# Query and key features stored feature first and head second, with one norm product for queries and one for keys per block

## The chip, the cores and the metric

The kernel runs on one core of one Trainium2 chip. A core has TensorE (PE in the profile, with its weight loads as PEld), VectorE (DVE), ScalarE (ACT), GpSimd (POOL) and SyncE (SP), which issues most DMAs. The metric is the device time of one execution in microseconds (us); the time of a kernel is the median of its runs.

## The reference

Two layers with the same weights act on 2048 tokens of 448 features: attention of 16 heads of 28 features, then a gated unit of 1792 features, each behind a layer norm without parameters and each added to its input.

```python
B, S, D, H, F = 1, 2048, 448, 16, 1792
def _A_ref(x, wqkv, wo):
    Dh = D // H                                           # 28
    qkv = (x @ wqkv).reshape(B, S, 3, H, Dh).transpose(2, 0, 3, 1, 4)
    q, k, v = qkv[0], qkv[1], qkv[2]
    scores = jnp.einsum("bhqd,bhkd->bhqk", q, k) * (Dh ** -0.5)
    o = jnp.einsum("bhqk,bhkd->bhqd", _softmax(scores), v)
    return o.transpose(0, 2, 1, 3).reshape(B, S, D) @ wo
def _B_ref(x, w_gate, w_up, w_down):
    return (_sigmoid(x @ w_gate) * (x @ w_up)) @ w_down
for layer in range(2):
    x = x + _A_ref(_layernorm(x), wqkv, wo)
    x = x + _B_ref(_layernorm(x), w_gate, w_up, w_down)
```

The columns of `wqkv` are ordered query, key, value; within each the head comes first and the feature within the head second. All inputs are float32.

## The kernel before

**Stages.** Each layer has a projection (`project`), the attention of 16 heads, the output projection and the gated unit. The change lies in the projection, and in the reads and writes that connect it to the weights before it and the heads behind it.

**Order of work.** Nothing plans the order at run time. Each engine executes its instructions in the order in which the program issues them, and waits on semaphores for its operands, so a waiting instruction holds all that stand behind it on its engine. The author interleaves work by hand: lists of small functions (`fill`, `along`, `along_values`) say what is issued between one tile and the next.

**Precision.** Activations and weights are kept as pairs of f16, a high part and the rest. A product of float32 quality is made of three f16 products: high by high, high by low, low by high.

**The projection's queries and keys.** The tokens come in 4 blocks of 512 (`W`). In a block, `qk` makes the 896 query and key features in 7 tiles of 128 features: tiles 0 to 2 hold queries, tile 3 holds the last 64 query features and the first 64 key features, tiles 4 to 6 hold keys. For each tile, `by_features` (L564) issues eleven matmuls of 512 columns into one of four PSUM banks. Then ScalarE writes the high part (L756), VectorE the low part (L757), both into `qkhl`; ScalarE squares the high part into `sq`, in bf16 (L759); VectorE takes the maximum of the left and right half of the 512 tokens (L761), which leaves 256 columns; and SyncE stores `qkhl` to `qk_scr` in DRAM (L764).

**The norms.** The softmax uses a bound from the largest norms of queries and keys. The squares of the 28 features of a head are summed by a product with a table of zeros and ones, `ind`. With the head first, every tile has features of other heads, so each tile has its own columns of the table: four products gather the query norms in one bank (L735) and four the key norms in another (L738), tile 3 going into both. The products stand in a queue `late`. From the fourth tile on, the oldest is issued behind the current tile's matmuls:

```python
if len(late) == 3:
    late.popleft()()
```

so those of tile 2 stand behind tile 5. The rest are issued by `finish` (`fin()`), in blocks 0 and 1 behind a value product, in block 2 between the first tiles of block 3, in block 3 behind the first value product that follows it. `finish` also reduces the two banks to `peaks` on VectorE. `tables` builds `ind` on GpSimd.

**The value products** (L589 to L591) follow the tiles of blocks 0 and 1; those of blocks 2 and 3 follow block 3's tiles. Beside all of it the norms of later blocks are computed on VectorE (`norm`, `squares`, `scale` at L320), their rows are transposed through DRAM and loaded back (`gather`), and split into parts (`ready`: the high part at L218 on ScalarE, the low one at L219 on VectorE). Block 1 of layer 0 is transposed on TensorE instead (L508, `turn`), behind VectorE's scaling at L320.

**The weights.** In layer 0 the weights come as float32 and are split on the chip: `high_cols` scales and rounds columns on ScalarE (L231), `low_cols` makes the rest on VectorE (L234). A power of two for the scale comes from a sum of squares (`measure`, `size`, with `powers` at L246 and L248). The first query columns are split before the first tile, the others between the first tiles of block 0 (`tile0`, `tile1`, `tile2`). The parts are written to DRAM (`keep`) and read back for layer 1 (`load`), so layer 1 splits nothing.

**The heads.** `HeadOperands.load` (L681 to L689) reads a head's 28 features from `qk_scr`, both parts of queries and keys, in several transfers on SyncE's queue. The scores are products of these rows (L1207).

Of the kernel before, what the change touches and what calls it, by code (L numbers as in the profile page):

```python
# [118 lines left out]
def interleaved_layers(ctx: ExitStack, tc: tile.TileContext, x_in, wqkv, wo, w_gate, w_up,  # L119
# [39 lines left out]
    ind_f = qrt.get("ind_f", [P, 8, H])  # L159
# [27 lines left out]
    def tables():  # L187


        nc.gpsimd.memset(ind_f, 1.0)  # L190
        for j in range(2):
            v = ind_f[:, 4 * j:4 * j + 4, :]
            off = -64 * j
            nc.gpsimd.affine_select(out=v, in_=v, compare_op=ALU.is_ge, fill=0.0, base=off,
                                    pattern=[[P, 4], [-DH, H]], channel_multiplier=1)
            nc.gpsimd.affine_select(out=v, in_=v, compare_op=ALU.is_ge, fill=0.0,
                                    base=DH - 1 - off, pattern=[[-P, 4], [DH, H]],
                                    channel_multiplier=-1)
        nc.gpsimd.memset(ind[:, 8:, :], 0.0)
        nc.gpsimd.tensor_copy(ind[:, 0:8, :], ind_f)  # L200
        qrt.put(ind_f)
# [24 lines left out]
    def scaled_high(hi, raw, m, engine=None):  # L226
        by = up[:, m:m + 1]
        if engine is nc.vector:
            nc.vector.tensor_scalar(hi, raw, by, None, op0=ALU.mult)
        else:  # L230
            nc.scalar.activation(hi, raw, AF.Copy, scale=by)  # L231
# [368 lines left out]
    class WeightsQKV:  # L600
# [37 lines left out]
            nc.tensor.matmul(pb[:, 0:1], ones, sums[:, j:j + 1], start=True, stop=True)  # L638
            powers(j, 1, pb[:, 0:1])

        def high_cols(self, j, c0, c1, kts=slice(0, 4)):
            c = slice(j * D + c0, j * D + c1)
            scaled_high(self.qk[0][:, kts, c], self.raw[j][:, kts, c0:c1], j)

        def low_cols(self, j, c0, c1):
            c = slice(j * D + c0, j * D + c1)
            scaled_low(self.qk[1][:, :, c], self.qk[0][:, :, c], self.raw[j][:, :, c0:c1], j)

        def split_v(self):
            for kts in (slice(0, 2), slice(2, 4)):  # L650
# [13 lines left out]
            nc.sync.dma_start(self.v, v_parts)  # L664


    qk_scr = dpool.tile([2 * D, 2, S], F16, name="qk_scr")
    g_scr = dpool.tile([H, 2, S], F16, name="g_scr")

    class HeadOperands:  # L670
# [8 lines left out]
        def load(self):  # L679
            h, q, k = self.h, self.q, self.k  # L680
            nc.sync.dma_start(k[RQ:RG, :], unit_scr)  # L681
            qs = qk_scr[h * DH:(h + 1) * DH]
            ks = qk_scr[D + h * DH:D + (h + 1) * DH]
            both = "d c n -> (d c) n"
            nc.sync.dma_start(q[0:2 * DH, :], qs.rearrange(both))
            nc.sync.dma_start(k[0:2 * DH, :], ks.rearrange(both))
            nc.sync.dma_start(q[2 * DH:RQ, :], qs.rearrange(both))
            nc.sync.dma_start(k[2 * DH:RQ:2, :], ks[:, 1, :])
            nc.sync.dma_start(k[2 * DH + 1:RQ:2, :], ks[:, 0, :])  # L689

        def load_guard(self):
            nc.sync.dma_start(self.q[RQ:RG, :], g_scr[self.h])
# [19 lines left out]
    def project(layer, wq, begun):  # L712
# [12 lines left out]
        def qk(b, blk, fill, before):  # L725
            pn = [bank(4 + 2 * (b % 2), "qnorm"), bank(5 + 2 * (b % 2), "knorm")]
            late = deque()

            def rows_of_heads(i):

                return ind[:, i:i + P // H, :].rearrange("p a h -> p (a h)")

            def norm_products(i, sq):
                if i <= 3:
                    nc.tensor.matmul(pn[0][:, 0:W // 2], rows_of_heads(i), sq[:, 0:W // 2],  # L735
                                     start=(i == 0), stop=(i == 3))
                if i >= 3:
                    nc.tensor.matmul(pn[1][:, 0:W // 2], rows_of_heads(1 + i), sq[:, 0:W // 2],  # L738
                                     start=(i == 3), stop=(i == 6))
                qrt.put(sq)  # L740

            for i in range(7):
                pm = bank(evac[0] % 4, "qkp")
                evac[0] += 1
                c = slice(i * P, (i + 1) * P)
                by_features(pm, blk, lambda kt: wq.qk[0][:, kt, c],
                            lambda kt: wq.qk[1][:, kt, c], i if layer == 0 and b == 0 else None)
                if layer == 0 and b == 0:
                    along[i]()
                if before and i in (1, 2):  # L750
                    before(i == 2)
# [4 lines left out]
                nc.scalar.activation(hl[:, 0, :], pm, AF.Copy, scale=PS)  # L756
                nc.vector.scalar_tensor_tensor(hl[:, 1, :], pm, PS, hl[:, 0, :], op0=ALU.mult,  # L757
                                               op1=ALU.subtract)
                nc.scalar.activation(sq, hl[:, 0, :], AF.Square)  # L759

                nc.vector.tensor_tensor(sq[:, 0:W // 2], sq[:, 0:W // 2], sq[:, W // 2:W],  # L761
                                        op=ALU.max)
                n = slice(b * W, (b + 1) * W)
                nc.sync.dma_start(qk_scr[c, :, n], hl)  # L764
                qrt.put(hl)
                late.append(lambda i=i, sq=sq: norm_products(i, sq))
                if i < len(fill) and fill[i]:
                    fill[i]()

            def finish(whole=True):  # L770

                while len(late) > (0 if whole else 1):
                    late.popleft()()
                for i in range(2 if whole else 0):
                    nc.vector.tensor_reduce(peaks[:, i, b:b + 1], pn[i][0:H, 0:W // 2], axis=AX.X,
                                            op=ALU.max)
            return finish
# [19 lines left out]
                blk.drop()  # L797

        def tile0():
            wq.low_cols(0, P, D)  # L800
            wq.measure(1)
            ones_of_values()

        def tile1():
            wq.size(1)
            wq.high_cols(1, 0, 64)
            wq.low_cols(1, 0, 64)

        def tile2():
            wq.high_cols(1, 64, D)  # L810
            wq.low_cols(1, 64, D)

        def nothing():
            pass
# [1039 lines left out]
    wq.sum_first(2)  # L1854
    tables()
    keep_busy(3)
    wq.high_cols(0, 0, P, slice(0, 1))
    wq.high_cols(0, 0, P, slice(1, 4))
    first.turned_high([3])
    wq.high_cols(0, P, D)  # L1860
    first.turned_low([1])
    wq.low_cols(0, 0, P)
    first.turned_low([2, 3])
    big.put(first.xn)
    qrt.put(still)
# [40 lines left out]
```

## Time and profile before

| | |
|---|---|
| median of 3 runs | 1894.67 us (1894.47 to 1895.89) |
| profiled execution, its span | 1893.0 us; the page gives it by its span alone |
| TensorE, matmuls | 1886.5 us busy |
| TensorE, weight loads | 1323.1 us |
| VectorE | 1430.7 us |
| ScalarE | 1382.7 us |
| GpSimd | 231.5 us |

The profile is one execution, recorded by the hardware profiler. The page gives busy times by engine and by group of instructions; a group's row has the line, the engine, the operation, output and inputs with their shapes, the count, then busy time, mean duration in ns, and the idle time of the engine just before with what ended it. The rows of the timeline begin with the start in us from the start of the span and a duration; `x3` at the end says that three neighbouring instructions were merged into one row, and a bracket says how long the engine had waited, and for which instruction. Matmuls overlap, so a matmul's duration is longer than the step to the next one.

### The profile page before, as it was taken

Reading aid. Unit: us, or ns where it says so; the run is one execution under the profiler, and the core shown is the slowest. Engines: PE = TensorE matmul, PEld = TensorE weight load, DVE = VectorE, ACT = ScalarE, POOL = GpSimd, SP = SyncE. Lnnn points to the kernel's source line nnn. Section 1 sums busy time; section 2 is a strip of 40 time slices with the busy share of each in tenths; the row PEclk is TensorE's granted clock in tenths of the full one; section 3 lists DMA queues with packets and bytes.
Section 4 is the critical chain, followed back from the end, with each engine's and each line's share of the span. In section 5 each row is a group of like instructions: output and inputs, shape, how many; then the busy total and the mean of one; then the engine's idle time right before and its main releaser. Section 6 shows DMA issues by size and latency. Waiting matters only on the chain. (4 is left out here: it accounts for less than half of the span.)

```text
span 1893.0 us, 56282 instructions
## 1 busy us (share of the span) xinstructions
PE 1886.5 (100%) x24254; PEld 1323.1 (70%) x24254; DVE 1430.7 (76%) x2835; ACT 1382.7 (73%) x1772; POOL 231.5 (12%) x453
## 2 busy tenths in 40 slices
PE   9999999999999999999999999999999999999999
PEld 4455555555556799999954556667666567999998
DVE  7758989898976688787564487787778676887664
ACT  5569999999993566555345799999999745565541
POOL 3023112222101111111100000000000020121110
PEclk9999999999999999999999999999999999999999
DMA  7676454334323566646734322122120245666553
GB/s 247 194 212 166 132 137 128 107 119 129 103 88 121 192 205 235 231 181 238 251 96 134 90 52 47 32 52 52 31 48 24 67 160 174 218 251 223 208 208 142
DMA packets 110882, 270.86 MB, mean 143 GB/s; under 512 B 13214, under 2 KB 67838, under 8 KB 110496
## 3 DMA queue, kind: packets, MB, share of 16 engines
q0 software_dynamic: 31776, 158.51, 23.4%
q1 hardware_dynamic: 78288, 108.20, 20.3%
q8 instruction: 192, 3.15, 0.7%
q10 hardware_dynamic: 560, 0.46, 0.1%
q14 instruction: 66, 0.54, 0.1%
HBM read 207.88 MB, written 50.85 MB: 137 GB/s over the span
## 5 line engine op out<-in xcount | busy, mean ns | idle before, releaser
L1222 ACT ACTIVATE prob_s<-sc 128x1536 f32<-128x1536 f32 (+1 forms) x657 | 887.9, 1487 | 6.6 <-PE sc L1207 5.9
L1258 PE MATMUL acc<-prob_s,val_s 128*32 128x256 f32 (+3 forms) x7700 | 569.9, 383 | 0.0
L1207 PE MATMUL sc<-qp_s 114*32 114x512 f16 x7868 | 553.2, 379 | 0.0
L579 PEld LDWEIGHTS <-gu_s 128*128 128x128 f16 x4368 | 426.9, 98 | 46.8 <-issue 0.4
L1207 PEld LDWEIGHTS <-qp_s 114*32 114x32 f16 x8192 | 272.7, 95 | 203.4 <-issue 88.3
L1258 PEld LDWEIGHTS acc<-prob_s,val_s 128*32 128x32 f32 x7700 | 272.3, 110 | 142.9 <-issue 13.6
L579 PE MATMUL chain<-xwide_s,gu_s 128*128 128x256 f16 x2016 | 247.5, 273 | 0.0
L1552 PE MATMUL dnp<-dn_s,hparts_s 128*128 128x224 f16 x2016 | 225.2, 259 | 0.0
L1552 PEld LDWEIGHTS <-hparts_s 128*128 128x128 f16 x2016 | 194.0, 98 | 4.4
L1238 DVE SCALAR_TENSOR_TENSOR power_q<-power_q,expo_q 128x512 f32<-128x512 f32 x243 | 168.2, 692 | 8.3
L1625 ACT COPY one_q<-chain 128x256 f32<-128x256 f32 x224 | 82.4, 371 | 121.4 <-PE chain L579 120.8
L1641 DVE TENSOR_TENSOR one_q<-side,one_q 128x512 f32<-128x512 f32 x112 | 72.2, 686 | 101.8 <-PE side L579 101.5
L579 PE MATMUL side<-xshort_s,gu_s 128*128 128x256 f16 x1120 | 140.5, 273 | 0.0
L564 PE MATMUL qkp<-xhl_s,wqk_s 128*128 128x512 f16 x616 | 138.1, 379 | 0.7 <-ACT wqk_s L231 0.2
L564 PEld LDWEIGHTS <-wqk_s 128*128 128x128 f16 x616 | 60.1, 98 | 69.8 <-ACT wqk_s L231 1.1
L1437 POOL DMA_DIRECT2D gu_s<-gu_parts x104 | 56.0, 538 | 430.5 <-PE side L579 424.5
L1287 DVE STREAM_TRANSPOSE oturned_q<-acc 128x512 f32<-128x512 f32 x32 | 22.9, 716 | 97.1 <-PE acc L1258 96.9
L1258 PE MATMUL acc<-power_q,val_s 128*32 128x256 f32 (+3 forms) x300 | 94.2, 396 | 0.0
L579 PE MATMUL side<-xwide_s,gu_s 128*128 128x256 f16 x672 | 91.6, 273 | 0.0
L1505 ACT CAST hparts_s<-hsums_q 128x256 f16<-128x256 f32 (+1 forms) x136 | 65.0, 494 | 30.2 <-DVE hsums_q L1517 20.2
L756 ACT ACTIVATE qkhl_q<-qkp 128x512 f16<-128x512 f32 x56 | 33.2, 593 | 71.9 <-PE qkp L564 68.3
L1652 ACT ACTIVATE one_q<-one_q 128x512 f32<-128x512 f32 x56 | 35.2, 629 | 64.3 <-DVE one_q L1641 64.3
(218 smaller groups left out, 2318.0 us busy)
## 6 DMA issues: line engine op xcount, KB each, us to landing
gu_s<-gu_parts POOLq DMA_DIRECT2D x104, 800.0 KB, 6.0
dn_s<-dn_parts POOLq DMA_DIRECT2D x42, 784.0 KB, 7.8
qp_s<-qk_scr SPq DMA_DIRECT2D x96, 224.0 KB
qk_scr<-qkhl_q SPq DMA_DIRECT2D x56, 256.0 KB
gu_parts<-pack_s POOLq DMA_DIRECT2D x14, 800.0 KB, 3.8
xt_scr<-xs_s SPq DMA_DIRECT2D x48, 224.0 KB
xraw_s<-xt_scr SPq DMA_DIRECT2D x12, 768.0 KB
qp_s<-qk_scr SPq DMA_DIRECT2D x64, 112.0 KB
```

The source lines that it names most:

```text
L564: nc.tensor.matmul(pm, w, x, start=(i == 0), stop=(i == len(terms) - 1))
L579: nc.tensor.matmul(pm, a, x, start=(first and i == 0), stop=(i == len(terms) - 1), skip_group_check=True)
L1207: nc.tensor.matmul(ps[32 * j:32 * j + 32, :], hd.k[:, keys], hd.q[:, qb * W:(qb + 1) * W], start=True, stop=True, tile_position=(0, 32 * j))
L1222: nc.scalar.activation(prob[:, 0:n, :], ps[:, 0:n, :], AF.Exp, scale=exp_scale)
L1238: nc.vector.scalar_tensor_tensor(p, p, c[k], y, op0=ALU.add, op1=ALU.mult)
L1258: nc.tensor.matmul(acc[qb * VC:(qb + 1) * VC, s], v[:, kc % TB, h, :], probs[c * NB + qb][:, s], start=(kc == 0 and a == 0), stop=(kc == N ...
L1437: queue.dma_start(self.gu[-1][m], gu_parts[p, m])
L1505: nc.scalar.copy(to[:, :, 0], a)
L1552: nc.tensor.matmul(pm, a[:, x, t], w[:, p, y], start=(begin and n == 0 and (j == 0 or alone)), stop=(n == 2), skip_group_check=True)
L1625: nc.scalar.copy(to, pm)
L1641: nc.vector.tensor_tensor(one[m], side[m], one[m], op=ALU.add)
L1652: nc.scalar.activation(out, v, AF.Sigmoid, scale=gate_scale)
```

## The change

Query and key features are stored with the feature first and the head second: row `d * 16 + h` instead of `h * 28 + d`. Every tile of 128 features then holds 8 features of all 16 heads, row r belonging to head r mod 16 in every tile, so the squares of several tiles can be added row by row before one product with one table.

- `ind` is one 128x128 table with the sums of heads in its first 16 columns; VectorE makes them from the identity matrix in one reduction (`sums_of_heads`) and GpSimd clears the rest.
- `squares_of` replaces `norm_products`. VectorE adds the squares of tiles 1, 2 and the query half of tile 3 to tile 0's, those of tiles 5 and 6 and the key half of tile 3 to tile 4's, over all 512 tokens; it takes the maximum of the two halves once for queries (tile 3) and once for keys (tile 6). One product for each follows. The query product is issued behind tile 5, the key product by `finish`.
- The weights of layer 0 are split with the same instructions, but read with a step of 28 words, and written in the new order; the low part is cut in four instructions, one for each 128 rows of weights. The first pieces are 8 features of 16 heads where 128 columns were.
- `qk_scr` is stored by query or key, part, row and token; tile 3 goes in two stores. A head's rows are 16 rows apart.

```diff
-    ind = cpool.tile([P, 7 + P // H, H], BF16, name="ind")
+    ind = cpool.tile([P, P], BF16, name="ind")
...
+    def sums_of_heads():
+        with nc.allow_low_precision(reason="zeros and a one"):
+            nc.vector.tensor_reduce(ind[:, 0:H], ident.rearrange("p (a h) -> p h a", h=H),
+                                    axis=AX.X, op=ALU.add)
...
-        def high_cols(self, j, c0, c1, kts=slice(0, 4)):
-            c = slice(j * D + c0, j * D + c1)
-            scaled_high(self.qk[0][:, kts, c], self.raw[j][:, kts, c0:c1], j)
-
-        def low_cols(self, j, c0, c1):
-            c = slice(j * D + c0, j * D + c1)
-            scaled_low(self.qk[1][:, :, c], self.qk[0][:, :, c], self.raw[j][:, :, c0:c1], j)
+        def columns(self, j, d0, d1, kts=slice(0, 4)):
+            c = j * D + (0 if j == 0 else -24 * H if d0 == 24 else 64)
+            c = slice(c + H * d0, c + H * d1)
+            hi, lo = [t[:, kts, c].rearrange("p k (d h) -> p k d h", h=H) for t in self.qk]
+            raw = self.raw[j][:, kts].rearrange("p k (h d) -> p k d h", h=H)[:, :, d0:d1]
+            return hi, lo, raw
+
+        def high_cols(self, j, d0, d1, kts=slice(0, 4)):
+            hi, lo, raw = self.columns(j, d0, d1, kts)
+            scaled_high(hi, raw, j)
+
+        def low_cols(self, j, d0, d1):
+            hi, lo, raw = self.columns(j, d0, d1)
+            for kt in range(4):
+                scaled_low(lo[:, kt], hi[:, kt], raw[:, kt], j)
...
-    qk_scr = dpool.tile([2 * D, 2, S], F16, name="qk_scr")
+    qk_scr = dpool.tile([2, 2, D, S], F16, name="qk_scr")
...
+            qs, ks = [rows[:, h] for rows in qk_scr.rearrange("w c (d h) n -> w (c d) h n", h=H)]
+            nc.sync.dma_start(q[0:2 * DH, :], qs)
...
-            def norm_products(i, sq):
-                if i <= 3:
-                    nc.tensor.matmul(pn[0][:, 0:W // 2], rows_of_heads(i), sq[:, 0:W // 2],
-                                     start=(i == 0), stop=(i == 3))
-                if i >= 3:
-                    nc.tensor.matmul(pn[1][:, 0:W // 2], rows_of_heads(1 + i), sq[:, 0:W // 2],
-                                     start=(i == 3), stop=(i == 6))
+            def norm_product(z, sq):
+                nc.tensor.matmul(pn[z][:, 0:W // 2], ind, sq[:, 0:W // 2], start=True, stop=True)
                 qrt.put(sq)
 
+            def squares_of(i, sq):
+                if i in (0, 4):
+                    sums["k" if i else "q"] = sq
+                    if i:
+                        both = sums.pop("both")
+                        nc.vector.tensor_tensor(sq[64:P], sq[64:P], both[64:P], op=ALU.add)
+                        qrt.put(both)
+                    return
+                z = 0 if i <= 3 else 1
+                to = sums["qk"[z]]
+                r = slice(0, 64 if i == 3 else P)
+                nc.vector.tensor_tensor(to[r], to[r], sq[r], op=ALU.add)
+                if i == 3:
+                    sums["both"] = sq
+                else:
+                    qrt.put(sq)
+                if i in (3, 6):
+                    nc.vector.tensor_tensor(to[:, 0:W // 2], to[:, 0:W // 2], to[:, W // 2:W],
+                                            op=ALU.max)
+                    late.append(lambda: norm_product(z, to))
...
-                if len(late) == 3:
+                if late and i in (2, 5):
                     late.popleft()()
...
-                nc.vector.tensor_tensor(sq[:, 0:W // 2], sq[:, 0:W // 2], sq[:, W // 2:W],
-                                        op=ALU.max)
+                squares_of(i, sq)
...
-                while len(late) > (0 if whole else 1):
+                while whole and late:
                     late.popleft()()
```

More of the change, by code (lines that the diff above doesn't have):

```diff
@@ L187, in tables @@
     def tables():
[L190 to L201, printed above, removed]
+        nc.gpsimd.memset(ind[:, H:], 0.0)
         units = big.get("units", [2, S], F16)
@@ L799, in tile0 @@
         def tile0():
-            wq.low_cols(0, P, D)
+            wq.low_cols(0, 8, DH)
+            sums_of_heads()
             wq.measure(1)
@@ L805, in tile1 @@
             wq.size(1)
[L806 to L807 removed]
+            wq.high_cols(1, 24, DH)
+            wq.low_cols(1, 24, DH)
         def tile2():
[L810 to L811 removed]
+            wq.high_cols(1, 0, 24)
+            wq.low_cols(1, 0, 24)
         def nothing():
```

32 lines of the change are left out of this document (15 added, 17 removed).

## The prediction

> **What bounds the kernel now.** I read the page first, then the matmul rows of the projection stage in order of time, then VectorE's rows of the same stretches, to see how far VectorE runs behind TensorE.
>
> ```profile
> span 1893.0 us, 56282 instructions
> PE 1886.5 (100%) x24254; PEld 1323.1 (70%) x24254; DVE 1430.7 (76%) x2835; ACT 1382.7 (73%) x1772; POOL 231.5 (12%) x453
> L735 PE MATMUL qnorm<-sq_q,ind 128*128 128x256 bf16 x32 | 8.7, 272 | 0.0
> L738 PE MATMUL knorm<-sq_q,ind 128*128 128x256 bf16 x32 | 6.4, 273 | 0.0
> ```
>
> TensorE is busy for all but 6.5 us of the span, so work taken off it shortens the kernel, and every wait put into its queue lengthens it. The page gives the profiled execution by its span, 1893.0 us; the median of the runs is 1.7 us above that. I work out a difference on the trace and add it to the median, 1894.67. About 0.2% (3.8 us) is what a measurement can tell from no change.
>
> There are 64 norm products, 8 for each of 4 blocks in 2 layers. What one costs is its step, not its duration, since matmuls overlap:
>
> ```profile
> 100.20 0.27 PE L735 MATMUL qnorm<-sq_q,ind 128*128 128x256 bf16 x1
> 102.68 0.27 PE L735 MATMUL qnorm<-sq_q,ind 128*128 128x256 bf16 x1
> 102.79 0.27 PE L738 MATMUL knorm<-sq_q,ind 128*128 128x256 bf16 x1
> 104.98 0.49 PE L738 MATMUL knorm<-sq_q,ind 128*128 128x256 bf16 x3
> ```
>
> From 102.68 to 102.79 is 0.11 us. The first row is the q product that follows feature tile 5 of block 3 in layer 0; the last holds the three k products that wait until the first value product is done.
>
> **Products.** 64 become 16: 48 x 0.109 = 5.2 us of TensorE, 2.6 in each layer. That is all that the change can give. What remains moves: the q product still stands behind tile 5, but now needs the sum over tiles 0 to 3, where the product there needed tile 2's squares. It is queued ahead of tile 6's eleven matmuls and all that follow.
>
> **VectorE's sums.** Seven maxima of 128x256 go; six adds of 128x512 (two of them on 64 partitions, which takes as long) and two maxima come in each block.
>
> ```profile
> 101.19 0.68 DVE L757 SCALAR_TENSOR_TENSOR qkhl_q<-qkp,qkhl_q 128x512 f16<-128x512 f32 x1
> 101.79 0.28 DVE L761 TENSOR_TENSOR sq_q<-sq_q 128x256 bf16<-128x256 bf16 x1
> 101.99 0.68 DVE L757 SCALAR_TENSOR_TENSOR qkhl_q<-qkp,qkhl_q 128x512 f16<-128x512 f32 x1
> L1516 DVE TENSOR_TENSOR hsums_q<-two_q,one_q 128x256 f32<-128x256 f32 x48 | 20.4, 425 | 1.6
> L761 DVE TENSOR_TENSOR sq_q<-sq_q 128x256 bf16<-128x256 bf16 x56 | 15.9, 284 | 0.0
> ```
>
> Back to back, an eviction holds the engine 0.60 us and a maximum 0.20. In bf16 256 columns last 284 ns, in f32 425, so bf16 goes at two elements a cycle, and a 512-column bf16 add should last 0.42 and hold the engine 0.33; with a maximum that depends on it behind, 0.45. So tile 0 gives VectorE 0.20 back, tiles 1, 2, 4 and 5 cost 0.13 each, tiles 3 and 6 cost 0.45: 1.2 us a block. The sum for q is ready 0.60 + 0.45 + 0.33 = 1.38 us after tile 3's eviction begins.
>
> **Where that meets TensorE.** VectorE's evictions of tile 3 in blocks 1 and 2 of layer 0 and block 1 of layer 1, and the q products behind tile 5:
>
> ```profile
> 58.02 0.65 DVE L757 SCALAR_TENSOR_TENSOR qkhl_q<-qkp,qkhl_q 128x512 f16<-128x512 f32 x1
> 83.47 0.69 DVE L757 SCALAR_TENSOR_TENSOR qkhl_q<-qkp,qkhl_q 128x512 f16<-128x512 f32 x1
> 992.03 0.69 DVE L757 SCALAR_TENSOR_TENSOR qkhl_q<-qkp,qkhl_q 128x512 f16<-128x512 f32 x1
> 56.89 0.27 PE L735 MATMUL qnorm<-sq_q,ind 128*128 128x256 bf16 x1
> 82.71 0.27 PE L735 MATMUL qnorm<-sq_q,ind 128*128 128x256 bf16 x1
> 993.80 0.27 PE L735 MATMUL qnorm<-sq_q,ind 128*128 128x256 bf16 x1
> 32.87 0.94 DVE L320 TENSOR_SCALAR xn_s<-x,mv,rs 128x448 f32<-128x448 f32 x2
> 33.48 1.66 PE L508 MATMUL turn<-ident,xn_s 128*128 128x128 f32 x8
> 37.07 1.04 PE L508 MATMUL turn<-ident,xn_s 128*128 128x128 f32 x8
> 64.31 0.68 DVE L757 SCALAR_TENSOR_TENSOR qkhl_q<-qkp,qkhl_q 128x512 f16<-128x512 f32 x1
> 79.85 1.29 DVE L219 TENSOR_TENSOR xhl_s<-xraw_s,xhl_s 128x512 f16<-128x512 f32 x2 [5.07 <-ACT xhl_s L218]
> ```
>
> In layer 0 VectorE carries the next blocks' norms between the evictions and runs late: at 56.89 TensorE stands behind tile 5 while tile 3's eviction only begins at 58.02. I follow the delay (after less before), the weights' reads being no dearer:
>
> - Block 0. The transposes (33.48, 1.66 us where the next take 1.04) wait for VectorE's scaling at 32.87. The sums of tiles 2, 3 and 5 lie in front of it, 0.13 + 0.45 + 0.13, with 0.04 of splitting (tile 4's hides in a wait for ScalarE): TensorE is 0.75 late there, and its four saved products are lost in the wait. Three k products become one: +0.53 at block 1.
> - Block 1. VectorE is 0.5 late, sum ready at 58.02 + 0.5 + 1.38 = 59.9. TensorE comes at 56.89 + 0.53 - 0.22 = 57.2: a wait of 2.6. Four more saved products leave +2.48 at block 2.
> - Block 2. VectorE resumes at 79.85 behind a transfer (ScalarE's copy of the reloaded rows) that follows tile 6's eviction at 64.31, 1.1 late after block 1's sums. Ready at 83.47 + 1.1 + 1.38 = 85.95, TensorE there at 82.71 + 2.48 - 0.22: wait 1.0, TensorE +3.24.
> - Block 3. Seven more tiles of sums make VectorE 2.3 late: 101.19 + 2.3 + 1.38 = 104.9 against 100.20 + 3.24 - 0.65 = 102.8: wait 2.05. Less four products, and some 0.15 for the k sum, which has only the 2.08 us from the q and k products to the k products (102.90 to 104.98) for eviction, add and maximum. Layer 0: **+4.35**.
> - Layer 1. Its 24 products give 2.62; VectorE has slack except in block 1, where tile 3's eviction comes 0.65 late: ready 994.06 against 993.80 - 0.87 = 992.93, wait 1.1, and 0.15 for the k sum. Layer 1: **-1.35**.
>
> After that TensorE is full and a delay passes to the end unchanged. So +3.0 us stands before the weights are counted.
>
> **Weights of layer 0.** Query and key weights are now read with a step of 28 f32 words, every element 112 bytes from the last, on ScalarE (L231) and VectorE (L234, cut in four: three more instructions at 0.06 each).
>
> ```profile
> 12.17 0.15 DVE L246 TENSOR_SCALAR pw<-sums 128x1 int32<-128x1 int32 x1
> 13.48 0.75 DVE L234 SCALAR_TENSOR_TENSOR wqk_s<-wraw_s,up,wqk_s 128x512 f16<-128x512 f32 x1 [0.38 <-ACT wqk_s L231]
> 15.59 1.54 DVE L234 SCALAR_TENSOR_TENSOR wqk_s<-wraw_s,up,wqk_s 128x1280 f16<-128x1280 f32 x1
> 17.37 0.69 DVE L757 SCALAR_TENSOR_TENSOR qkhl_q<-qkp,qkhl_q 128x512 f16<-128x512 f32 x1 [0.24 <-ACT qkhl_q L756]
> 18.72 0.16 DVE L246 TENSOR_SCALAR pw<-sums 128x1 int32<-128x1 int32 x1 [0.39 <-PE sums L638]
> 22.25 1.82 DVE L234 SCALAR_TENSOR_TENSOR wqk_s<-wraw_s,up,wqk_s 128x1536 f16<-128x1536 f32 x1 [1.17 <-ACT wqk_s L231]
> 12.54 0.91 ACT L231 ACTIVATE wqk_s<-wraw_s,up 128x128 f16<-128x128 f32 x2 [0.91 <-DVE up L248]
> 19.10 0.51 ACT L231 ACTIVATE wqk_s<-wraw_s,up 128x256 f16<-128x256 f32 x1 [1.10 <-DVE up L248]
> 20.66 1.56 ACT L231 ACTIVATE wqk_s<-wraw_s,up 128x1536 f16<-128x1536 f32 x1
> L1288 DVE RECIPROCAL rec<-oturned_q 128x16 f32<-128x16 f32 x32 | 8.1, 254 | 1.1
> ```
>
> These lie one after another ahead of the scaling that the transposes wait for: 384 (three of the first four parts), 1280 and 1536 elements on VectorE, 512, 256 and 1536 on ScalarE. Contiguous, VectorE takes (1.82 - 0.75)/1024 = 1.04 ns an element and ScalarE (1.56 - 0.51)/1280 = 0.82. No row shows such a step alone; the nearest is the division, 16 words with a step of 32: (254 - 150)/15 = 6.9 ns, and it divides too. So VectorE's price lies between 1.04 (a step cannot beat neighbours) and 6.9. I choose near the same instruction's row but not on it: VectorE twice its price, ScalarE, with one input, half as much again. That is 3200 x 1.04 = 3.3 plus 2304 x 0.41 = 0.95, less the 0.63 of VectorE's waits at 17.37 and 18.72 that this uses up: **+3.6**. At 6.9 ns it would be 18 us.
>
> [...]
>
> **No cost.** Eight more stores and denser loads on SyncE's queue: the first head's loads start long before its scores,
>
> ```profile
> 105.43 0.31 SPq L685 DMA_DIRECT2D qp_s<-qk_scr  x1
> 118.43 0.83 PE L1207 MATMUL sc<-qp_s 114*32 114x512 f16 x12
> ```
>
> 13 us apart, and both ends move together. Were loads from rows 64 KB apart to take 5 us longer, that would begin to show. The table on GpSimd goes; nobody waits for it, VectorE's 0.2 us reduction falls in the wait at 17.37.
>
> Sum: 4.35 - 1.35 + 3.6 = +6.6, **1901.3 us**.
>
> **Rivals.**
>
> Stepped reads at full rate (0.28): +3.0, 1897.7, in the 0.2%. For it: no row shows a step costing anything that the division would not explain. Against: no row shows one free.
>
> [...]
>
> Dearer sums or reads (0.12): adds at one element a cycle hold 0.60, and some fifteen on layer 0's path at 0.27 more give 4.0, with 0.5 in layer 1: 1905.8; reads at 2.5 times come out alike. Against: 284 to 425 ns above.
>
> Faster (0.10): the q sum is in time. Place: behind tile 5 of layer 0's blocks 1 to 3 and layer 1's block 1; it decides if tile 3's eviction begins 1.38 us before tile 5 ends. Then 20 products of layer 0 and 24 of layer 1 count, -4.8, against +0.75 in block 0: 1890.6. Against it stand the rows, 1.1 and 0.8 us on the wrong side. That the change doesn't do what it says can be ruled out: built, 16 products remain.
>
> **How the numbers follow.** Forecast 0.50, 1901.3, by itself 1899 to 1904. Full-rate reads fall mostly under 3.8 us (0.22 of 0.28), and 0.02 of the forecast does: same 0.24, slower 0.66, faster 0.10. The range, 1896.0 to 1906.0, leaves out the faster case and the far end of the reads.
>
> **What would show it.** TensorE idle before the q product of blocks 1 to 3 of layer 0, some 2.6, 1.0 and 2 us, released by VectorE's maximum; 1.1 in block 1 of layer 1; L234's four parts of 384 together about 3.4 us (1.9 at full rate); first scores near 126 instead of 118.43. If those idles are missing, the sum is wrong at its root; if the parts last 1.9 us, the first rival holds.

## The result, and the profile after

The changed kernel takes 1903.90 us (median of 5 runs, 1903.39 to 1905.58) where the kernel before takes 1895.43 beside it: 8.5 us more, a ratio of 1.0046 with a 95% interval of 1.0035 to 1.0057. The forecast was 6.6 us more, in a range that holds the result.

The first lines of the changed kernel's page, and two groups of instructions (line, engine, operation, tiles and shapes, count, then busy us, mean ns, idle us before with what ended it):

```profile
span 1901.9 us, 56255 instructions
PE 1884.7 (99%) x24206; PEld 1334.8 (70%) x24206; DVE 1446.6 (76%) x2856; ACT 1387.2 (73%) x1772; POOL 230.6 (12%) x447
L731 PE MATMUL qnorm<-sq_q,ind 128*128 128x256 bf16 x8 | 2.2, 271 | 5.9 <-DVE sq_q L752 5.9
L746 DVE TENSOR_TENSOR sq_q<-sq_q,sq_q 128x512 bf16<-128x512 bf16 (+1 forms) x40 | 16.6, 416 | 0.0
```

48 products are gone, and TensorE's busy time fell, from 1886.5 to 1884.7 us, while the span grew by 8.9. TensorE's idle time grew from 6.5 to 17.2 us, and 5.9 us of that stand ahead of the eight query products alone. The sums last 416 ns; the prediction had 0.42, its author's estimate from rows of 284 and 425 ns. No trace shows a rate in cycles.

The timeline of TensorE in the changed kernel, at the query products behind tile 5 in layer 0 (34.10 to 110.66) and in block 1 of layer 1, with block 0's wait for its transposes' input (40.50), the last of the very first transposes (11.00) and the first scores (128.66):

```profile
11.00 0.66 PE L502 MATMUL turn<-ident,xn_s 128*128 128x128 f32 x4 [1.00 <-DVE xn_s L314]
34.10 0.27 PE L731 MATMUL qnorm<-sq_q,ind 128*128 128x256 bf16 x1 [0.73 <-DVE sq_q L752]
40.50 1.71 PE L502 MATMUL turn<-ident,xn_s 128*128 128x128 f32 x8 [0.37 <-DVE xn_s L314]
66.25 0.27 PE L731 MATMUL qnorm<-sq_q,ind 128*128 128x256 bf16 x1 [2.56 <-DVE sq_q L752]
91.45 0.27 PE L731 MATMUL qnorm<-sq_q,ind 128*128 128x256 bf16 x1
110.66 0.27 PE L731 MATMUL qnorm<-sq_q,ind 128*128 128x256 bf16 x1 [2.21 <-DVE sq_q L752]
1004.25 0.27 PE L731 MATMUL qnorm<-sq_q,ind 128*128 128x256 bf16 x1 [0.45 <-DVE sq_q L752]
128.66 1.48 PE L1225 MATMUL sc<-qp_s 114*32 114x512 f16 x24
```

The waits forecast for blocks 1 and 3 (2.6 and 2.05 us) are there as 2.56 and 2.21, ended by VectorE's maximum. Block 2's (1.0) is missing, block 0's 0.73 was not forecast, and layer 1's is 0.45 where 1.1 was forecast. The first scores start 10.2 us later than before, at 128.66 where the prediction expected them near 126. The transposes behind block 0's first value product start 7.0 us later (33.48 before).

0.9 of both is there before the first tile: the fourth token tile's transposes start at 11.00, not 10.11. VectorE's scaling ahead of them, and GpSimd's memset of `units`, which stands behind the table's instructions in `tables`, in the kernel before and then in the changed one:

```profile
9.12 0.51 DVE L320 TENSOR_SCALAR xn_s<-x,mv,rs 128x448 f32<-128x448 f32 x1 [0.44 <-POOL rs L500]
10.93 1.79 POOL L203 MEMSET units_s<- 2x2048 f16 x1
```

```profile
8.85 2.09 DVE L314 TENSOR_SCALAR xn_s<-x,mv,rs 128x448 f32<-128x448 f32 x1 [0.44 <-POOL rs L494]
8.90 1.79 POOL L191 MEMSET units_s<- 2x2048 f16 x1
```

Without the old table's instructions on GpSimd, the memset starts 2 us earlier and falls on the scaling, which lasts 2.09 us instead of 0.51. So it is in all five traces with the change's start (the changed kernel, e1, e2, e3, e6: 2.09 to 2.10 us, the memset 0.05 us behind the scaling's start), and in none of the eight with the old start (0.51, the memset 1.8 us behind it). From the scaling's start to tile 0's first matmul the plain reads take 5.1 us in e2 and e3 and 3.9 in the kernel before, so this costs about 1.2 us there. No run separates it from the rest of the change.

The split of the query and key weights in the changed kernel, VectorE's four parts of 384 and ScalarE's 1536, and the block 1 rows that make the wait of 2.56:

```profile
26.98 3.43 DVE L228 SCALAR_TENSOR_TENSOR wqk_s<-wraw_s,up,wqk_s 128x384 f16<-128x384 f32 x4 [2.17 <-ACT wqk_s L225]
23.85 3.10 ACT L225 ACTIVATE wqk_s<-wraw_s,up 128x1536 f16<-128x1536 f32 x1
64.90 0.65 DVE L772 SCALAR_TENSOR_TENSOR qkhl_q<-qkp,qkhl_q 128x512 f16<-128x512 f32 x1
65.47 0.40 DVE L746 TENSOR_TENSOR sq_q<-sq_q,sq_q 64x512 bf16<-64x512 bf16 x1
65.91 0.29 DVE L752 TENSOR_TENSOR sq_q<-sq_q 128x256 bf16<-128x256 bf16 x1
```

3.43 us is what the prediction named as the sign of a dear read (3.4, against 1.9). ScalarE went from 1.56 to 3.10: twice as long, not half as much again. Tile 3's eviction, add and maximum run from 64.90, and the product follows at 66.25: 1.35 us, forecast 1.38.

### The profile page after: what moved, and what is told of

Read it like the earlier page. It is cut to its first block, busy times and chain, and to the rows that moved or that the text cites. A ratio compares the mean times of both kernels' runs of the same rounds, so it can differ in the third digit from the quotient of the medians.

```text
span 1901.9 us, 56255 instructions
## 1 busy us (share of the span) xinstructions
PE 1884.7 (99%) x24206; PEld 1334.8 (70%) x24206; DVE 1446.6 (76%) x2856; ACT 1387.2 (73%) x1772; POOL 230.6 (12%) x447
## 5 line engine op out<-in xcount | busy, mean ns | idle before, releaser
L1225 PEld LDWEIGHTS <-qp_s 114*32 114x32 f16 x8192 | 281.6, 96 | 195.8 <-issue 83.2
L1276 PEld LDWEIGHTS acc<-prob_s,val_s 128*32 128x32 f32 x7700 | 281.0, 110 | 135.3 <-issue 12.7
```

Source lines behind the costliest of these rows:

```text
L1225: nc.tensor.matmul(ps[32 * j:32 * j + 32, :], hd.k[:, keys], hd.q[:, qb * W:(qb + 1) * W], start=True, stop=True, tile_position=(0, 32 * j))
L1276: nc.tensor.matmul(acc[qb * VC:(qb + 1) * VC, s], v[:, kc % TB, h, :], probs[c * NB + qb][:, s], start=(kc == 0 and a == 0), stop=(kc == N ...
```

## The experiments

Every kernel was timed in five rounds beside the kernel before, whose medians there were 1895.11 (e1 to e4), 1895.55 (e5 to e7) and 1895.45 us (e9 to e11). Only the probe e8 was run once, for its durations. Each ratio's 95% interval reaches 1.7 to 2.9 us to either side, so a difference between two experiments is uncertain by 2 to 3 us. Where an expectation speaks of a replay, layer 0's instructions were gone through again in each engine's order with the durations and waits of the trace, with one duration, place or count changed.

### Where the loss sits: the query product's place, and the reads

**e1, the query product issued later.** The changed kernel with

```diff
-                if late and i in (2, 5):
-                    late.popleft()()
```

> The changed kernel with one edit: the query product is no longer issued behind tile 5, but by finish together with the key product. If the waits ahead of the query product (2.56, 2.21, 0.73 us in layer 0 and 0.45 us in layer 1 of the changed kernel's trace) are lost time in full, 5.9 us come back: about 1898. If VectorE's lateness is the true bound in layer 0, TensorE only meets it again at the next bank or value product, and a replay of the stage with the trace's durations gives back 1.4 us there and 0.5 in layer 1: about 1902. If the reads of the weights are the whole loss, nothing changes: 1903.9.

It took 1901.11 us (ratio to before 1.0034, 1.0021 to 1.0048), 2.8 us less than the changed kernel (2.5 if each is taken against the kernel before beside it). 5.9 us of waits were removed and under half came back. TensorE, let past the query product, met VectorE again a few instructions on. Its rows in block 3 and at block 1's value product:

```profile
68.96 0.35 PE L583 MATMUL vp<-wv_s,xhl_s 128*128 128x448 f16 x1 [0.98 <-DVE qkhl_q L770]
106.98 2.53 PE L558 MATMUL qkp<-xhl_s,wqk_s 128*128 128x512 f16 x11 [0.20 <-DVE qkhl_q L770]
113.34 0.27 PE L731 MATMUL knorm<-sq_q,ind 128*128 128x256 bf16 x1 [1.63 <-DVE sq_q L752]
```

The first two wait for a PSUM bank that VectorE has not yet emptied, the third for the key sum. So the wait's place is a part of the loss, and VectorE's lateness another.

**e2, plain reads.** The changed kernel with

```diff
-            raw = self.raw[j][:, kts].rearrange("p k (h d) -> p k d h", h=H)[:, :, d0:d1]
+            raw = self.raw[j][:, kts].rearrange("p k (d h) -> p k d h", h=H)[:, :, d0:d1]
```

> The changed kernel, but layer 0's query and key weights are read as neighbouring words; the features of heads are then mixed, so the output is another. Everything else is as in the changed kernel. If the step of 28 words doubles both engines' price per element (3.43 us for four parts of 384 on VectorE, 3.10 us for 1536 on ScalarE, where neighbours took 1.82 and 1.56) and lies on the path, a replay says 5.2 us come back: about 1898.7, and the first transposes of block 1 start near 35 us instead of 40.5. If the reads are hidden, 1903.9. At the 3.6 us of the prediction, 1900.3.

1899.02 us (1.0023, 1.0014 to 1.0032): 4.9 us less than the changed kernel (4.6 against the kernel before beside each). The same four parts on VectorE, and the transposes; ScalarE's 1536 take 1.56 again:

```profile
23.21 2.21 DVE L228 SCALAR_TENSOR_TENSOR wqk_s<-wraw_s,up,wqk_s 128x384 f16<-128x384 f32 x4 [0.81 <-ACT wqk_s L225]
35.50 1.71 PE L502 MATMUL turn<-ident,xn_s 128*128 128x128 f32 x8 [0.37 <-DVE xn_s L314]
```

The transposes start 5.0 us earlier than in the changed kernel, though the fourth token tile's had begun within 0.12 us of each other: the reads' price arises before 40 us and is paid to the end. Four parts of plain reads take 2.21 us where one instruction took 1.82 before, so the cut in four costs 0.39 by itself.

The query products of layer 0 wait 2.54 us in block 1 and 0.81 in block 3 here, and not at all in blocks 0 and 2; layer 1's waits 0.42. Behind the 2.54, TensorE's granted clock in this trace was 0.50 from 62 to 65 us, and eleven matmuls took 4.22 us where the changed kernel's took 2.54 at 1.00: 1.7 us of TensorE's time in this trace is that.

**e3, both edits.**

> Both edits of the two kernels before in one: reads of neighbouring words, and the query product issued by finish. What is left of the change is VectorE's sums, 48 products fewer, and the new storage. If sums on VectorE cost as much in layer 0 as the products saved, it comes out near the kernel before, 1896.5; if the waits of the query product and the reads were all that cost, it is 5 us faster than the kernel before: 1890.5.

1897.01 us (1.0010, 1.0001 to 1.0019). With plain reads and the query product out of the way, the change still costs 1.9 us over the kernel before, though 48 products are gone. A third cost remains.

**e4, stepped reads alone.** The kernel before, its reads changed as the change does:

```diff
-            scaled_high(self.qk[0][:, kts, c], self.raw[j][:, kts, c0:c1], j)
+            hi = self.qk[0][:, kts, c].rearrange("p k (d h) -> p k d h", h=H)
+            raw = self.raw[j][:, kts].rearrange("p k (h d) -> p k d h", h=H)
+            scaled_high(hi, raw[:, :, c0 // H:c1 // H], j)
...
-            scaled_low(self.qk[1][:, :, c], self.qk[0][:, :, c], self.raw[j][:, :, c0:c1], j)
+            hi, lo = [t[:, :, c].rearrange("p k (d h) -> p k d h", h=H) for t in self.qk]
+            raw = self.raw[j].rearrange("p k (h d) -> p k d h", h=H)[:, :, c0 // H:c1 // H]
+            for kt in range(4):
+                scaled_low(lo[:, kt], hi[:, kt], raw[:, kt], j)
```

> The kernel before with one edit: the query and key weights of layer 0 are read with a step of 28 words, in the same pieces as before, the low parts cut in four. The heads' features are mixed, so the output is another. If the reads cost by themselves what the plain reads give back, 5.2 us: about 1900.6. If they cost only together with VectorE's sums, under 3 us: below 1898.5.

1900.69 us (1.0027, 1.0016 to 1.0038), 5.6 more than before, the cut in four included, which e2 keeps. The reads cost as much without the sums as with them, within the intervals; they are a loss of their own.

### What 48 products are worth, and what the sums cost

**e5, 48 products left out, nothing added.**

```diff
-                if i <= 3:
-                    nc.tensor.matmul(pn[0][:, 0:W // 2], rows_of_heads(i), sq[:, 0:W // 2],
-                                     start=(i == 0), stop=(i == 3))
-                if i >= 3:
+                if i == 3:
+                    nc.tensor.matmul(pn[0][:, 0:W // 2], rows_of_heads(i), sq[:, 0:W // 2],
+                                     start=True, stop=True)
+                if i == 6:
...
```

> The kernel before with 48 of its 64 norm products left out (one for queries and one for keys of a block remain, over the squares of tiles 3 and 6 alone), so the bound on the norms is not the reference's use of them; nothing is added on VectorE. If TensorE alone sets the pace of both projections, all of it comes back: 48 x 0.109 = 5.2 us, about 1889.9. If layer 0 is paced by VectorE's evictions as well, a replay of its stage gives 0.9 us there, and layer 1 2.6: about 1891.6.

1891.94 us (0.9982, 0.9973 to 0.9991): 3.6 us less, not 5.2. ScalarE's evictions of the last tile of layer 0 and of the first and last tile of layer 1, in the kernel before and then in e5:

```profile
102.88 0.60 ACT L756 ACTIVATE qkhl_q<-qkp 128x512 f16<-128x512 f32 x1 [1.23 <-PE qkp L564]
956.10 0.60 ACT L756 ACTIVATE qkhl_q<-qkp 128x512 f16<-128x512 f32 x1 [28.84 <-PE qkp L564]
1039.79 0.60 ACT L756 ACTIVATE qkhl_q<-qkp 128x512 f16<-128x512 f32 x1 [1.23 <-PE qkp L564]
```

```profile
101.75 0.60 ACT L756 ACTIVATE qkhl_q<-qkp 128x512 f16<-128x512 f32 x1 [1.11 <-PE qkp L564]
955.13 0.60 ACT L756 ACTIVATE qkhl_q<-qkp 128x512 f16<-128x512 f32 x1 [28.83 <-PE qkp L564]
1036.53 0.60 ACT L756 ACTIVATE qkhl_q<-qkp 128x512 f16<-128x512 f32 x1 [1.11 <-PE qkp L564]
```

The lead over the kernel before is 1.1 us at the end of layer 0's tiles and grows from 1.0 to 3.3 within layer 1. (At the first tile's eviction e5 was 0.16 us behind: 16.92 against 16.76.) So layer 1 pays in full (2.3, and the products behind the last tile), layer 0 about half of its 2.6.

From e5 to e3 it is 5.5 us: 1897.01 less 1891.94, plus the 0.4 between the two medians of before. In between lie the sums, and with them what e3 keeps of the change besides: the long scaling at the start (about 1.2), the cut in four, the storage in two parts. In the traces e3 is 5.0 us behind e5 at layer 1's first eviction (960.14 against 955.13) and 5.0 at its last (1041.55 against 1036.53): the cost arises before layer 1, and layer 1 takes its sums without loss. How much of it is the sums alone, no run shows; by the 1.2, some 4 us at most, an estimate.

Why layer 0 pays only in part stands in one row, the busy times in 80 to 105 us, blocks 2 and 3 of layer 0. The kernel before (length, then busy us and count of TensorE, its weight loads, VectorE, ScalarE, GpSimd; then clock, DMA share, GB/s), and under it a stretch in layer 1:

```profile
80.00:105.00 25.00, 25.00 (x125) 12.04 (x124) 24.60 (x51) 16.58 (x29) 0.00 (x0) 1.00 0.33 111
980.00:1005.00 25.00, 25.00 (x127) 12.25 (x126) 13.99 (x30) 12.14 (x22) 0.00 (x0) 1.00 0.70 197
```

In layer 0 VectorE is busy for 24.60 of 25 us, as TensorE is; in layer 1 for 13.99. The page's 76% is a mean over such stretches. If two engines that are both full pace the stage together, neither alone gives much when it is relieved. Three kernels test this.

**e9, VectorE lightened.** The kernel before without the maxima in layer 0:

```diff
-                nc.vector.tensor_tensor(sq[:, 0:W // 2], sq[:, 0:W // 2], sq[:, W // 2:W],
-                                        op=ALU.max)
+                if layer > 0:
+                    nc.vector.tensor_tensor(sq[:, 0:W // 2], sq[:, 0:W // 2], sq[:, W // 2:W],
+                                            op=ALU.max)
```

> The kernel before without VectorE's seven maxima a block in layer 0 (1.4 us of VectorE in each block; the norms then see the left 256 tokens of a block alone). If VectorE alone paced layer 0, up to 5.6 us would go: about 1890. If TensorE alone does, nothing: 1895.4. If both run at nearly one pace there, a replay gives 0.6 us: about 1894.8.

1894.67 us (0.9996, 0.9987 to 1.0005). By time alone this can't be told from no change; it excludes the 5.6 us expected if VectorE alone set the pace.

**e10, both lightened:** e5's and e9's edits together.

> Both lightened: 48 norm products left out in both layers, and the seven maxima a block left out in layer 0. With the products alone left out the time was 1891.94. If the two engines pace layer 0 together, what neither gives alone comes out when both are lightened: a replay gives 2.8 us in layer 0 instead of 0.9, so about 1890.1. If layer 0 is held by something else, 1891.9 stays, or 1891.3 with the maxima's own 0.6.

1890.04 us (0.9972, 0.9960 to 0.9983), 5.4 less than before. Products alone gave 3.6, maxima alone 0.8; together a little more than their sum, by 1.0 us, which is within the intervals. The replay had said 3.5 for the products alone and 5.4 for both; that the two engines hold each other is supported by this and not proved.

**e11, VectorE burdened.** The kernel before with

```diff
-                nc.vector.tensor_tensor(sq[:, 0:W // 2], sq[:, 0:W // 2], sq[:, W // 2:W],
-                                        op=ALU.max)
+                for _ in range(2 if layer == 0 and i > 0 else 1):
+                    nc.vector.tensor_tensor(sq[:, 0:W // 2], sq[:, 0:W // 2], sq[:, W // 2:W],
+                                            op=ALU.max)
```

> The kernel before with six of the seven maxima of each block in layer 0 taken twice: 1.2 us more of VectorE in each block, the amount that the sums add, and nothing else; products and their places stay, and the result is the same. If the sums cost by their load on VectorE alone, a replay gives 2.5 us: about 1897.9. If VectorE has that much room, as a busy share of 76% would suggest, no change: 1895.4. If all of it lay on the path, 4.8: 1900.2.

1899.29 us (1.0019, 1.0010 to 1.0028): 3.8 us more. The expectation took 0.20 us for each added maximum, 4.8 in all. But the second maximum needs the first one's result, and the pair holds VectorE 0.52 us, from its start to the next instruction's, where one maximum held it 0.20:

```profile
99.20 0.60 DVE L762 TENSOR_TENSOR sq_q<-sq_q 128x256 bf16<-128x256 bf16 x2
99.72 1.14 DVE L959 CUSTOM_DVE_ANT_0 junk_s<-raw_s,sums 128x896 bf16<-128x896 f32 x1
```

So VectorE was given 24 x 0.32 = 7.7 us, and about half came out at the end (1.9 to 5.3 by the interval); the replay had half of 4.8. No product was added or moved. VectorE has some room in layer 0, but far less than its 76% suggests. TensorE in block 3 of layer 0, where it had no wait before (the first is ended by ScalarE's eviction, the second by the added maximum):

```profile
99.86 0.28 PE L735 MATMUL qnorm<-sq_q,ind 128*128 128x256 bf16 x1 [0.67 <-ACT qkhl_q L756]
102.89 0.28 PE L735 MATMUL qnorm<-sq_q,ind 128*128 128x256 bf16 x1 [0.38 <-DVE sq_q L762]
```

### Other ways to the new order

**e6, read in order and written with a step.** The changed kernel with

```diff
-            hi, lo = [t[:, kts, c].rearrange("p k (d h) -> p k d h", h=H) for t in self.qk]
-            raw = self.raw[j][:, kts].rearrange("p k (h d) -> p k d h", h=H)[:, :, d0:d1]
+            hi, lo = [t[:, kts, c].rearrange("p k (d h) -> p k h d", h=H) for t in self.qk]
+            raw = self.raw[j][:, kts].rearrange("p k (h d) -> p k h d", h=H)[:, :, :, d0:d1]
```

> The changed kernel with one edit: the weights' split walks the heads outermost and the features innermost, so that the float32 words are read as neighbours (runs of 8, 20, 24 or 4) and the f16 results are written with a step of 16 elements; the low part also reads the high part with that step. The result is the same. If only the stepped float32 read is dear, the time is that of the plain reads, about 1899. If any step of one operand is dear, it stays at 1903.9; if two stepped operands cost more than one, above it.

1918.75 us (1.0122, 1.0107 to 1.0138), 15 us worse than the change. The splits grew, but they may not be all of it: TensorE's granted clock was 0.83 from 10 to 40 us and 0.74 from 40 to 60 here, and 1.00 in the changed kernel. What each is worth isn't shown. ScalarE's 1536 and three of VectorE's parts of 384:

```profile
31.05 6.78 ACT L225 ACTIVATE wqk_s<-wraw_s,up 128x1536 f16<-128x1536 f32 x1
37.86 5.12 DVE L228 SCALAR_TENSOR_TENSOR wqk_s<-wraw_s,up,wqk_s 128x384 f16<-128x384 f32 x3 [5.61 <-ACT wqk_s L225]
```

With stepped f16 writes an element takes 4.4 ns on both engines, about twice as long as with stepped reads (2.2 on VectorE, 2.0 on ScalarE). VectorE's low part also reads the high part with a step here; the probe writes with a step and reads in order.

**e8, a probe of steps.** The kernel before, with instructions of 448 elements behind its end (each step twice):

```python
for s in (1, 2, 4, 8, 16, 28, 56):              # read f32 with a step of s words
    nc.vector.scalar_tensor_tensor(los_in_order, src.rearrange("p (a s) -> p s a", s=s), by,
                                   his_in_order, op0=ALU.mult, op1=ALU.subtract)
for s in (2, 4, 16, 28):                        # write f16 with a step of s
...                                             # and scaled copies of both kinds on ScalarE
```

> The kernel before with instructions behind its end that do nothing for the result, for their durations alone: 448 elements each, float32 read with a step of 1, 2, 4, 8, 16, 28 and 56 words, or f16 written with a step of 2, 4, 16 and 28, on ScalarE (scaled copy) and VectorE (the low part's operation). If the price comes from leaving neighbours at all, a step of 2 costs as much as 28, some 2.2 ns an element on VectorE and 1.9 on ScalarE; if it grows with the distance, it rises from 2 to 28.

VectorE: f32 reads with steps 1, 2, 4, 28; then f16 writes with steps 2, 4, 16. ScalarE: reads with steps 1, 2, 4, 28; then a write with step 16:

```profile
1891.55 0.69 DVE L1887 SCALAR_TENSOR_TENSOR prlo_s<-prsrc_s,up,prhi_s 128x448 f16<-128x448 f32 x1
1892.27 0.69 DVE L1887 SCALAR_TENSOR_TENSOR prlo_s<-prsrc_s,up,prhi_s 128x448 f16<-128x448 f32 x1
1893.71 1.00 DVE L1887 SCALAR_TENSOR_TENSOR prlo_s<-prsrc_s,up,prhi_s 128x448 f16<-128x448 f32 x1
1900.93 1.02 DVE L1887 SCALAR_TENSOR_TENSOR prlo_s<-prsrc_s,up,prhi_s 128x448 f16<-128x448 f32 x1
1904.75 0.72 DVE L1892 SCALAR_TENSOR_TENSOR prlo_s<-prsrc_s,up,prhi_s 128x448 f16<-128x448 f32 x1
1906.75 1.21 DVE L1892 SCALAR_TENSOR_TENSOR prlo_s<-prsrc_s,up,prhi_s 128x448 f16<-128x448 f32 x1
1907.99 2.09 DVE L1892 SCALAR_TENSOR_TENSOR prlo_s<-prsrc_s,up,prhi_s 128x448 f16<-128x448 f32 x1
1865.87 0.67 ACT L1879 ACTIVATE prlo_s<-prsrc_s,up 128x448 f16<-128x448 f32 x1
1867.31 0.70 ACT L1879 ACTIVATE prlo_s<-prsrc_s,up 128x448 f16<-128x448 f32 x1
1869.18 1.10 ACT L1879 ACTIVATE prlo_s<-prsrc_s,up 128x448 f16<-128x448 f32 x1
1875.94 1.11 ACT L1879 ACTIVATE prlo_s<-prsrc_s,up 128x448 f16<-128x448 f32 x1
1885.83 2.25 ACT L1883 ACTIVATE prlo_s<-prsrc_s,up 128x448 f16<-128x448 f32 x1
```

Neither expectation held. For reads, a step of two words costs next to nothing (0.69 us as at one on VectorE, 0.70 against 0.67 on ScalarE), four cost nearly the full price (1.00 and 1.10), and little more is added up to 56 (1.04 and 1.13): a cliff, on both engines alike. A read past it adds (1.02 - 0.69)/448 = 0.7 ns an element on VectorE and (1.11 - 0.67)/448 = 1.0 on ScalarE.

For f16 writes the price is there at a step of four too, 1.21 us on VectorE where two took 0.72, and it goes on rising, to 2.09 at 16. What in the hardware makes either, the probe doesn't show; it gives the durations.

**e7, the sums in layer 1 alone, and no stepped split.** The kernel before in layer 0. In layer 1 the weights stay stored head first and TensorE loads every seventh column, so a tile holds four features of all heads of queries and keys:

```diff
+                c = c if layer == 0 else slice(i, 2 * D, 7)
                 by_features(pm, blk, lambda kt: wq.qk[0][:, kt, c],
...
+                if layer == 1 and i > 0:
+                    nc.vector.tensor_tensor(total[0], total[0], sq, op=ALU.add)
...
+            def products_of_sum(sq):
+                for z in range(2):
+                    nc.tensor.matmul(pn[z][:, 0:W // 2],
+                                     ind[:, 8 * z:8 * z + 8].rearrange("p a h -> p (a h)"),
+                                     sq[:, 0:W // 2], start=True, stop=True)
```

> The kernel before in layer 0. In layer 1, weight loads of TensorE take every seventh column of the weights as stored head first, so that each tile has four features of all heads of queries and of keys; VectorE adds the squares of all seven tiles, and finish issues the two norm products. The rows in DRAM stay as before. If a weight load with a step of 7 f16 columns stays under the 216 ns of a matmul, and VectorE's sums find room in layer 1, 8 products become 2 in each block: 24 x 0.109 = 2.6 us less, about 1892.7, and less than the kernel before. If a stepped load takes over 216 ns, 308 matmuls are paced by it: at 300 ns, 26 us slower.

1892.87 us (0.9985, 0.9976 to 0.9994): 2.7 us less than the kernel before and 11 less than the change; it is the version to keep. The weight loads of layer 1's query and key matmuls, first in the kernel before and then here (953 to 1047 us), and the 24 adds, six in each block:

```profile
L564 PEld LDWEIGHTS <-wqk_s 128*128 128x128 f16 x308 | 30.1, 98 | 34.2
L564 PEld LDWEIGHTS <-wqk_s 128*128 128x128 f16 x308 | 40.5, 132 | 25.6
L778 DVE TENSOR_TENSOR sq_q<-sq_q,sq_q 128x512 bf16<-128x512 bf16 x24 | 10.1, 420 | 0.0
```

A stepped load lasts 132 ns instead of 98, beside matmuls that follow each other every 215 ns (e1's row of eleven, 2.53 us less the last one's 0.38, over ten steps), and stays hidden. 24 adds of 0.42 us find room: in the layer 1 stretch above, VectorE was busy for 14 of 25 us.

## Why the prediction was right, and where its terms were off

The direction, and the two mechanisms that made it, held: the weights' reads cost on the path, and the query product waits for VectorE in layer 0. In medians, each against before in its own comparison: 48 products -3.6 (e5), the sums with what else e3 keeps of the change +5.5 (e3 less e5), the query product's place behind tile 5 +2.0 (e2 less e3), the stepped reads +4.6 (the change less e2). These are steps of one chain of kernels, so they add up to the 8.5 by construction; that is no proof of any of them. Each difference is uncertain by 2 to 3 us, so the 2.0 is shown by the waits in the traces and not by the times.

- **Without the reads**, layers 0 and 1 were to cost +3.0 together; e2 measured 3.9. The part was near, its split was not, and that is in part luck. The waits of 2.6, 1.0, 2.05 and 1.1 us came as 2.54, none, 0.81 and 0.42 in e2: 3 us too much was forecast. (By its own numbers the first is 59.9 less 57.2, so 2.7.) In their place stand costs that the sum doesn't have: block 1's transposes start 2.0 us late where 0.75 was forecast (35.50 against 33.48), of which 0.8 is there by the first eviction (17.59 against 16.76) and so ahead of any sum, and in the profiled execution 1.7 us went with the lower clock.
- **Block 2's wait** of 1.0 came neither in e2 nor in the changed kernel. There VectorE starts again when the reloaded rows are split, and in the changed kernel that start moved by less than TensorE: by 6.6 us, from 79.85 to 86.44. ScalarE's evictions of tiles 1 and 2 of block 2, before and then after:

```profile
73.19 0.60 ACT L756 ACTIVATE qkhl_q<-qkp 128x512 f16<-128x512 f32 x1 [1.12 <-PE qkp L564]
80.24 0.59 ACT L756 ACTIVATE qkhl_q<-qkp 128x512 f16<-128x512 f32 x1
```

```profile
82.11 0.60 ACT L771 ACTIVATE qkhl_q<-qkp 128x512 f16<-128x512 f32 x1 [1.12 <-PE qkp L558]
86.83 0.59 ACT L771 ACTIVATE qkhl_q<-qkp 128x512 f16<-128x512 f32 x1
```

Tile 1's is 8.9 us later than before, tile 2's only 6.6 (in e2 5.6 and 1.0). So the sum was ready when TensorE came, if barely: VectorE's maximum in the changed kernel ends at 91.40, and the product starts at 91.45:

```profile
91.11 0.29 DVE L752 TENSOR_TENSOR sq_q<-sq_q 128x256 bf16<-128x256 bf16 x1
```

- **Layer 1** was to give 1.35; it gave 1.8 (its first eviction moved from 956.10 to 966.80, 10.7 us, and the end of the span by 8.9). Its one wait was 0.45 and not 1.1, which is more than the difference.
- **The reads** were the mis-sized term: +3.6 forecast, 4.6 to 5.6 measured. The step that failed is ScalarE at "half as much again": it is twice (1.56 to 3.10 us). VectorE was taken at twice and is at 1.7 to 1.8 times (0.7 to 0.8 ns added to 1.04), and the cut costs 0.39 us on 1536 columns where the author's estimate was three instructions at 0.06. That VectorE's four parts came out at 3.43, as forecast, hid that: 1.82, 0.39 for the cut and 1.22 for the step. With the measured prices the same sum gives 3200 x 0.79 + 2304 x 1.00 - 0.63 = 4.2.
- **"5.2 us is all that the change can give"** was an upper bound, and right as one; 3.6 is what the products are worth here. An earlier sentence, that work taken off TensorE shortens the kernel since it is busy for all but 6.5 us, holds only in part in layer 0, where e5 gained 1.1 to 1.3 us of 2.6. The prediction met this block by block and drew no general conclusion from it.
- **The rivals.** Full-rate reads are refuted by the probe and by e4. The faster case failed by its condition, a query sum in time (waits of 2.56 and 2.21). Taking the product out of the sum's way doesn't bring it back either: e3 removes both that wait and the reads, and is not below the kernel before.
- **The table on GpSimd** was put at nothing: "The table on GpSimd goes; nobody waits for it". That nobody waits for the table is right. But its going lets the memset of `units` start 2 us earlier, on VectorE's scaling, and tile 0's first matmul came about 1.2 us late for it. That the memset is what holds the scaling is inferred from thirteen traces; no kernel moved the memset alone. A term of this size is missing from the forecast, which fell 1.9 us short.

## What to carry to other kernels

Read each engine's busy share in the stage that changes, not over the span: an engine at 76% of the span was at 98% in the stage that received the sums, and there about half of the work that e11 put on it came out at the end. A reordering that spares one engine can land on another, so look for the engine that can do it behind cover: here VectorE and ScalarE cost 4.6 to 5.6 us by stepped reads on the path, TensorE's weight loads did a like reordering in 34 ns more each, hidden under matmuls. Place work by stage: the sums cost time in layer 0 and none in layer 1. And when work is taken off an engine that nobody waits for, look at what moves up into its place.

## What the runs showed of the hardware

- f32 reads from SBUF with a step of 2 words are as fast as neighbours on VectorE and nearly so on ScalarE (0.69 and 0.70 us for 448 elements in e8, neighbours 0.69 and 0.67); from 4 words on they cost 0.7 and 1.0 ns more an element, about the same at 4, 28 and 56 (1.00, 1.02 and 1.04 us on VectorE, 1.10, 1.11 and 1.13 on ScalarE).
- Stepped f16 writes are dearer than stepped reads from a step of 4 on: for 448 elements in e8 VectorE takes 0.72 us at a step of 2, 1.21 at 4 and 2.09 at 16 (reads 1.00 at 4 and 0.96 at 16), ScalarE 1.30 at 4 and 2.25 at 16 (reads 1.10 and 1.07); in e6 both took 4.4 ns an element.
- A weight load of TensorE whose columns are 14 bytes apart lasts 132 ns instead of 98 (e7).
- VectorE's scaling of 128x448 f32 lasted 2.09 to 2.10 us in the five traces where a GpSimd memset of 1.79 us began 0.05 us behind it, and 0.51 in the eight where it didn't.
- TensorE's granted clock fell to 0.50 for some 3 us behind a wait of 2.54 us in e2, and stayed at 1.00 behind one of 2.56 us in the changed kernel.
